# Wider weight slices, gates ahead of values, and earlier loads in a fused attention and SwiGLU kernel

## The chip, the cores and the metric

The kernel runs on one core of one Trainium2 chip. The metric is the device time of one execution in microseconds; lower is better. The core has PE (matmul; PEld is its weight load), DVE, ACT, POOL and SP. SP and POOL issue the DMAs here, and 16 DMA engines serve both queues.

## The reference

The input has 8 batches, 8 heads, 576 positions and a head size of 64. The attention is linear: q gets a softmax over the head size and k one over the sequence; `kv` is k transposed times v; and the output is q times `kv`. The result, 4608 tokens of 512 columns, goes through a gated feed-forward layer with 1536 hidden columns.

```python
q_s = np.exp(q); q_s = q_s / np.sum(q_s, axis=-1)       # softmax, maxima left out here
k_s = np.exp(k); k_s = k_s / np.sum(k_s, axis=2)
x = einsum('bhsd,bhde->bhse', q_s, einsum('bhsd,bhse->bhde', k_s, v))   # -> 4608 x 512
g = x @ w_gate
out = (g * sigmoid(g) * (x @ w_val)) @ w_out
```

Inputs and the output are float32.

## The kernel before

**Weights.** `w_slice` and `wo_slice` load the three weight matrices with DMAs issued from POOL; on the way, the DMA turns float32 into float16. The gate and value weights come in column slices (256, 256, 512 and 512), a slice of the gate and then the same slice of the value matrix. Then w_out comes in three slices of four row tiles of 128. They are listed in `w_dma`, and the first waits for v of batch 0.

**Attention.** A batch is two groups (G) of four heads. `load` brings q, k or v of one group to SBUF from SP's queue, 576 KB each. `exp` is an activation on ACT (`eq`, `ek`). `norm_sum` (`ns`) sums on DVE, `norm_mul` multiplies by the reciprocals on POOL (`nm`, `nd` with a star) or DVE. `tr` transposes on PE for batches 0 and 1; `tr_dma` does it by a DMA for the later ones. `cast_v` (`cv`) turns v into bf16. `kv` and `kv_kn` (`kk`) form the small matrix and scale it, and `x` (`xz`) or `x_pair` (`xx`) write x, transposed, into the ring `xt`.

**Feed-forward layer.** The tokens of batch 0 (576) are done plainly, by class `First`: step `I m` is the gate product of column tile m (eight matmuls into two PSUM banks, 320 and 256 tokens) and its silu on ACT; step `J m` is the value product and the multiply on DVE that writes the hidden ring `hr`. `Unit` (`O j 1`, `O j 2`) multiplies 128 tokens with the first and second half of w_out. The other tokens come in chunks: one of 448 (`PLAN_0`), then seven of 512. There, four pairs of column tiles (`a` to `g`, with `v`) use Strassen's scheme with seven products in the place of eight; the sums of weights are made by `g_sum` (`Q`, `T`) and `w_sum` (`W`), those of x by `x_sum` (`X`, `Y`). The remaining tiles are plain (`G m` gate, `U m` value). The product with w_out of the chunk before is made by `Quad` (`A` to `H`), with sums of `hr` (`S`, by `h_sum`). In the last chunks six pairs are used and no plain tiles.

**What sets the order.** The whole runs under a manual schedule: the order in the program is the order on each engine's queue, and each engine works its queue in order. The order is written out by hand in plan strings: `PLAN_B` (batch 0's layer, attention of batch 1 and the start of batch 2), `PLAN_0` (the 448 tokens), `PLAN` (chunks 1 to 5), `PLAN_N` (6 and 7) and `PLAN_E` (the last product). `op` reads a token, and `chunk` walks a plan. A star moves part of a step to another engine: for `a`, `c`, `d` the copy from ACT to DVE, for `e` and `g` the multiply from POOL to DVE, for `nm` and `Q` from POOL to DVE, for `nd`, `X`, `Y` and `W` from DVE to POOL. `silu` is a tiny activation that brings ACT's table in ahead of its use.

**Buffers.** The PSUM pool `psp` has eight banks, one tile each. The pool `ff` has four buffers `sg` for silu results. `ld` has three buffers for q and k and two for v. `add_manual_dep` adds a wait between two DMAs: before, q of batch 1 waits for `w_dma[-3]`, the first slice of w_out, and k, v of batch 1 and all of batch 2, group 0, follow it on SP's queue.

Of the kernel before, what the change touches and what calls it, by code (L numbers as in the profile page):

```python
# [8 lines left out]
FP32 = mybir.dt.float32  # L9
BF16 = mybir.dt.bfloat16  # L10
FP16 = mybir.dt.float16
AF = mybir.ActivationFunctionType
SYNC = mybir.DependencyInfo(mybir.DependencyClass.Sync, mybir.DependencyReason.DATA)
# [3 lines left out]
def kernel(  # L17
# [19 lines left out]
    nc = tc.nc  # L37

    B, H, S, D = q.shape
# [17 lines left out]
    ff = ctx.enter_context(tc.tile_pool(name="ff", bufs=4))  # L57
# [7 lines left out]
    wg = const.tile([128, KT, d_ff], FP16, name="wg", tag="wg")  # L65
    wv = const.tile([128, KT, d_ff], FP16, name="wv", tag="wv")
# [6 lines left out]
    hr = const.tile([128, MT, RING], BF16, name="hr", tag="hr")  # L73
# [6 lines left out]
    def load(b, G, what, src, after=None):  # L80
        raw[what, b, G] = ld.tile(
            [128, 2, T * 64], FP32, tag=what, name=what, bufs=2 if what == "v" else 3
        )
        ap = bass.AP(
            tensor=src.tensor,
            offset=src[b, 4 * G].offset,
            ap=[[T * 64, 128], [2 * HSTR, 2], [1, T * 64]],
        )
        d = nc.sync.dma_start(out=raw[what, b, G], in_=ap)
        if after is not None:  # L90
            tc.add_manual_dep(d.ins, after.ins.name, SYNC, reason="order of loads")
        dmas[what, b, G] = d
# [5 lines left out]
    def w_slice(dst, src, c0, n):  # L98
        ap = bass.AP(
            tensor=src.tensor,  # L100
            offset=src[0, c0].offset,
            ap=[[d_ff, 128], [128 * d_ff, KT], [1, n]],
        )
        return nc.gpsimd.dma_start(out=dst[:, :, c0:c0 + n], in_=ap)  # L104

    def wo_slice(m0, n):
        ap = bass.AP(
            tensor=moe_w_out.tensor,
            offset=moe_w_out[m0 * 128, 0].offset,
            ap=[[d_model, 128], [128 * d_model, n], [1, d_model]],  # L110
        )
        return nc.gpsimd.dma_start(out=wo[:, m0:m0 + n, :], in_=ap)
# [9 lines left out]
    A, Z = BANKS = ((0, 5), (5, 9))  # L122
# [130 lines left out]
    def warm_up(n):  # L253
        ps = f_tile("warm_ps")
        for _ in range(n):
            nc.tensor.matmul(
                out=ps[:, 0:256], lhsT=zero[:, 0:128], rhs=zero, start=True, stop=True
            )
# [41 lines left out]
    class First:  # L300
# [14 lines left out]

        def run(self, step, alt=False):
            if step == "I":
                self.sg = []
                for p_, (c, n) in zip(self.mm(wg, "g_ps"), self.parts):
                    self.sg.append(ff.tile([128, 512], FP32, tag="sg", name="sg"))  # L320
                    nc.scalar.activation(out=self.sg[-1][:, 0:n], in_=p_[:, 0:n], func=AF.Silu)
            else:
                for p_, sg, (c, n) in zip(self.mm(wv, "u_ps"), self.sg, self.parts):
                    nc.vector.tensor_mul(hr[:, self.m, c:c + n], sg[:, 0:n], p_[:, 0:n])

    def g_cols(w, kh, c0, c1):
        return w[:, 2 * kh:2 * kh + 2, :].rearrange("p k (j c) -> p k j c", j=2)[:, :, :, c0:c1]
# [22 lines left out]
            eng.tensor_sub(s[3], a12, s[1])  # L350

    def sg_tile():
        return ff.tile([128, 512], FP32, tag="sg", name="sg")

    class Pair:
        def __init__(self, c0, h, n, tsum, tc0):
# [35 lines left out]
        def run(self, step, alt=False):  # L392
# [7 lines left out]
            elif step == "b":  # L400
                self.y = f_tile("sy")
                self.prod(self.y, self.raw(wg, 1), self.xa(0, 1), True)
            elif step == "c":
                self.w, self.s5 = f_tile("sw"), self.s_tile("s5")
                self.prod(self.w, self.sum(0), xs[0], True)
                copy(ceng, self.s5, self.w[:, 0:w])
            elif step == "v":
                nc.vector.tensor_add(self.s1, self.y[:, 0:w], self.s1)  # L408
                self.sa = sg_tile()
                nc.scalar.activation(out=self.sa[:, 0:w], in_=self.s1, func=AF.Silu)  # L410
            elif step == "d":
                self.s2 = self.s_tile("s2")
                self.prod(self.x, self.sum(1), xs[1])
                copy(ceng, self.s2, self.x[:, 0:w])
            elif step == "e":
                self.prod(self.w, self.raw(wv, 1), xs[3])
                nc.vector.tensor_add(self.s2, self.w[:, 0:w], self.s2)  # L417
                meng.tensor_mul(self.out(0), self.halves(self.sa), self.halves(self.s2))  # L418
            elif step == "f":
                self.prod(self.x, self.sum(2), xs[2])  # L420
                nc.vector.tensor_add(self.s5, self.x[:, 0:w], self.s5)  # L421
            elif step == "g":
                self.prod(self.x, self.sum(3), self.xa(1, 1))
                sb = sg_tile()
                nc.scalar.activation(out=sb[:, 0:w], in_=self.x[:, 0:w], func=AF.Silu)  # L425
                meng.tensor_mul(self.out(1), self.halves(sb), self.halves(self.s5))  # L426

    class Direct:
# [13 lines left out]
        def run(self, step, alt=False):  # L442
            n = self.n
            if step == "G":
                ps = self.mm(wg, "g_ps")
                self.sg = sg_tile()
                nc.scalar.activation(out=self.sg[:, 0:n], in_=ps[:, 0:n], func=AF.Silu)
            else:
                ps = self.mm(wv, "u_ps")
                nc.vector.tensor_mul(  # L450
                    hr[:, self.m, self.rh:self.rh + n], self.sg[:, 0:n], ps[:, 0:n]
                )
# [141 lines left out]
    with tc.manual_schedule():  # L594
# [20 lines left out]
        cast_v(0, 0, nc.scalar)  # L615

        w_dma = []
        for c0, n in ((0, 256), (256, 256), (512, 512), (1024, 512)):
            w_dma.append(w_slice(wg, moe_w_gate, c0, n))
            w_dma.append(w_slice(wv, moe_w_val, c0, n))  # L620
        tc.add_manual_dep(w_dma[0].ins, dmas["v", 0, 0].ins.name, SYNC, reason="order of loads")
        for m0 in (0, 4, 8):
            w_dma.append(wo_slice(m0, 4))

        warm_up(WARM[0])
        for G in range(NG):
# [17 lines left out]
        x(0, 1, A)  # L644
        x(0, 1, Z)

        load(1, 0, "q", q, after=w_dma[-3])
        load(1, 1, "q", q)
        for G in range(NG):
            load(1, G, "k", k)  # L650
            load(1, G, "v", v)
        load_group(2, 0)

# [88 lines left out]
        ORDER = (0, 1, 2, 3, 4, 5)  # L742
        gt2 = [None] * 4
        PLAN_B = """
        I0 J0 I1 I2 J1 J2 I3 J3 I4 I5 J4 J5 I6 I7 J6 I8 Q0* J7 J8 I9 I10 Q2* Q1* J9 eq0:1
        Q3 J10 eq1:1 I11 ns0:1 ns1:1 J11 ek0:1 ek1:1 nd1:1 O01 nd0:1* cv0:1 O11 O02* tr00
        cv1:1 O12 tr10 tr11 kk0:1 eq0:2 cv0:2 load:2 tr01 O21 xz00 kk1:1 xz01* ns0:2 O22
        nm0:2 ek0:2 xz10* O31 cv1:2 xz11 eq1:2 O32 ek1:2
"""
        PLAN_0 = """  # L750
        a0 b0 ns1 load v0 Y0 G4 a1 Y2 Y1* kv U4 c0 d0 G10 f0 b1 c1 Y3 nm1 W0 g0 d1 v1 a2
        e0 f1 e1 b2 c2 g1 d2 W1 v2 U10 a3 f2 G5 b3 g2 v3 e2 c3 d3* xx* e3 U5 f3 W2 X0 X2
        X1 G11 U11 g3* X3 W3
"""
        PLAN = """
        S002 G4 S022 S102 a0 b0 G10 d0 c0 A v0 a1 S042 eq0 S122 S142 S302 B S342 f0 S242
        b1 ek0 U4 S322 D S222 ek1 e0 eq1 cv0 S202 C* v1 cv1 g0 ns0 F E d1 H* a2 ns1 c1 f1
        silu nm0 b2 c2 nm1 e1 g1 d2* v2 a3 U10 f2 e2 load kv b3 g2 c3 d3 G5 v3 e3* f3 xx*
        X0 G11 U5 X1 U11 g3* X3 X2
"""  # L760
        PLAN_N = """
        a0 b0 c0 d0 A v0 T0* f0 S002 a1 b1 g0 d1 c1 S022 S102 S222 v1 e0 a2 S202 f1 e1 b2
        S042 c2 g1 d2 v2 S122 B f2 a3 T1 b3 c3 S242 S142 g2 e2 d3 S322 D v3 a4 f3 T2 C g3
        T3 d4 b4 e3 c4 v4 f4 S302 F a5 g4 b5 S342 d5 v5 e4 c5* f5 E X0 X1 e5* X3 X2* g5*
        H*
"""
        PLAN_E = """
        S202 S042 S022 S002 A S142 S122 S102 B C S322 S302 S342 D S222 S242 E F H*
"""
        chunk(-1, 0, S, PLAN_B)  # L770
        chunk(0, S, 1024 - S, PLAN_0)
# [33 lines left out]
```

## Time and profile before

| what | value |
|---|---|
| median of 5 runs | 302.82 us (301.5 to 304.96) |
| profiled execution, its own time | 304.12 us |
| its span | 302.2 us |
| PE, PEld, DVE, ACT, POOL busy | 290.9, 228.4, 232.4, 210.7, 136.7 us |
| HBM read and written | 37.75 and 9.44 MB |
| q0 (POOL's DMAs), q1 (SP's) | 4.72 and 41.30 MB |

The span is the time between the first and the last record of the profiled execution. Its own time is longer by what lies around the span. A busy time of an engine is the sum of its instructions' times without overlaps. The traffic of q0 is counted as written, in float16, which is half of what is read.

### The profile page before, as it was taken

The page shows a single profiled execution, that of the slowest core. Times are in us where ns is not written, and L with a number is a line of the kernel's source. Part 1 is how long each engine was busy: PE and PEld are TensorE (multiplying, and loading weights), DVE is VectorE, ACT ScalarE, POOL GpSimd, SP SyncE. Part 2 cuts the span into 40 slices and gives each one's busy share as a digit, 9 for nine tenths or more (in the row PEclk, how much of TensorE's full clock was granted, in tenths as well). Part 3 has the DMA queues.
Part 4 walks back from the last instruction along what each step waited for, and adds up shares of the span by engine and source line. Part 5 has one row for each costly group of instructions (what it writes and reads, how often), then busy time and mean ns, then how long its engine had stood idle before and what let it go on. Part 6 is the DMA issues. An engine that isn't in the chain of part 4 may idle for free.

```text
span 302.2 us, 6895 instructions
## 1 busy us (share of the span) xinstructions
PE 290.9 (96%) x2644; PEld 228.4 (76%) x2644; DVE 232.4 (77%) x497; ACT 210.7 (70%) x385; POOL 136.7 (45%) x108
## 2 busy tenths in 40 slices
PE   8999978979999999999999999999999999999993
PEld 6777744558688858885888588858886888888882
DVE  3943846658898878887888788878988898895981
ACT  5654377677889488948894889488948776567540
POOL 1840155456407910791079107910794465274500
PEclk9999997979999999999999999999999999999999
DMA  7999998999001993189317941993190000600066
GB/s 268 267 179 206 236 395 286 303 293 293 0 3 34 177 359 120 34 176 343 139 32 158 335 165 31 190 341 129 30 192 0 0 2 4 135 7 0 2 139 139
DMA packets 38863, 46.43 MB, mean 154 GB/s; under 512 B 16304, under 2 KB 21936, under 8 KB 38832
## 3 DMA queue, kind: packets, MB, share of 16 engines
q1 hardware_dynamic: 33024, 41.30, 47.6%
q0 software_dynamic: 5808, 4.72, 10.2%
q8 instruction: 20, 0.33, 0.5%
q14 instruction: 11, 0.09, 0.1%
HBM read 37.75 MB, written 9.44 MB: 156 GB/s over the span
## 4 chain that ended last, share of the span: by engine, by line
PE 79%; DMA 13%; POOL 2%; SPq 1%; ACT 1%; DVE 1%; issue 0%; ACTq 0%; POOLq 0%; DVEq 0%
PE sx L384 21%; PE ox L526 14%; PE sw L384 10%; PE u_ps L435 7%; PE ow L526 7%; PE g_ps L435 7%; DMA wo<-in_moe_w_out_dram 5%; DMA v<-in_v_dram 5%; PE sy L384 5%; PE oy L526 3%; DMA q<-in_q_dram 2%; PE kv L192 2%; POOL wg L104 1%; PE o_ps L473 1%; POOL wv L104 1%; DVE rs L143 1%
## 5 line engine op out<-in xcount | busy, mean ns | idle before, releaser
L418 POOL TENSOR_TENSOR hr<-sg,s 128x512 bf16<-128x512 f32 (+1 forms) x29 | 38.0, 1309 | 74.7 <-DVE s L417 73.5
L384 PEld LDWEIGHTS <-gt 128*128 128x128 f16 x576 | 56.6, 98 | 11.0 <-issue 0.7
L426 POOL TENSOR_TENSOR hr<-sg,s 128x512 bf16<-128x512 f32 (+1 forms) x28 | 35.7, 1274 | 36.9 <-ACT sg L425 36.9
L384 PE MATMUL sx<-xs,gt 128*128 128x256 f16 (+1 forms) x288 | 43.1, 273 | 0.0
L116 ACT COPY s<-sx 128x512 f32<-128x512 f32 (+1 forms) x66 | 38.2, 579 | 5.2 <-PE sx L384 4.4
L526 PEld LDWEIGHTS <-hs 128*128 128x128 bf16 x384 | 37.6, 98 | 5.4
L417 DVE TENSOR_TENSOR s<-sw,s 128x512 f32<-128x512 f32 (+1 forms) x36 | 24.5, 681 | 16.5 <-PE sw L384 16.2
L425 ACT ACTIVATE sg<-sx 128x512 f32<-128x512 f32 (+1 forms) x36 | 21.2, 590 | 19.9 <-PE sx L384 14.7
L152 POOL TENSOR_TENSOR qs<-eq,rr 128x1152 bf16<-128x1152 bf16 x14 | 29.5, 2127 | 11.4 <-DVE rr L147 11.4
L421 DVE TENSOR_TENSOR s<-sx,s 128x512 f32<-128x512 f32 (+1 forms) x36 | 24.4, 679 | 10.0 <-PE sx L384 4.8
L384 PEld LDWEIGHTS <-wg 128*128 128x128 f16 x288 | 27.7, 98 | 5.2
L526 PEld LDWEIGHTS <-hr 128*128 128x128 bf16 x288 | 28.1, 98 | 3.3
L143 DVE TENSOR_REDUCE rs<-eq 128x18 f32<-128x1152 bf16 x16 | 21.5, 1341 | 10.0 <-ACT eq L127 10.0
L410 ACT ACTIVATE sg<-s 128x512 f32<-128x512 f32 (+1 forms) x36 | 22.5, 626 | 8.0 <-DVE s L408 7.9
L116 ACT COPY s<-sw 128x512 f32<-128x512 f32 (+1 forms) x34 | 19.8, 584 | 9.9 <-PE sw L384 4.9
L408 DVE TENSOR_TENSOR s<-sy,s 128x512 f32<-128x512 f32 (+1 forms) x36 | 24.3, 674 | 1.3 <-ACT s L116 0.8
L435 PE MATMUL g_ps<-xt,wg 128*128 128x512 f16 (+1 forms) x96 | 24.5, 378 | 0.0
L435 PE MATMUL u_ps<-xt,wv 128*128 128x512 f16 (+1 forms) x96 | 24.1, 384 | 0.0
L526 PE MATMUL ox<-wt,hs 128*128 128x256 f16 x192 | 23.6, 273 | 0.0
L384 PE MATMUL sw<-xs,gt 128*128 128x256 f16 (+1 forms) x144 | 21.8, 275 | 0.0
L384 PE MATMUL sy<-xt,wg 128*128 128x256 f16 (+1 forms) x144 | 21.4, 271 | 0.0
L384 PE MATMUL sx<-xt,gt 128*128 128x256 f16 (+1 forms) x144 | 21.4, 271 | 0.0
(99 smaller groups left out, 570.8 us busy)
## 6 DMA issues: line engine op xcount, KB each, us to landing
q<-in_q_dram SPq DMA_DIRECT2D x16, 576.0 KB, 6.7
k<-in_k_dram SPq DMA_DIRECT2D x16, 576.0 KB, 8.0
v<-in_v_dram SPq DMA_DIRECT2D x16, 576.0 KB, 8.6
out_dram<-o_sb SPq DMA_DIRECT2D x72, 128.0 KB, 2.4
wo<-in_moe_w_out_dram POOLq DMA_DIRECT2D x3, 512.0 KB, 18.4
wg<-in_moe_w_gate_dram POOLq DMA_DIRECT2D x2, 512.0 KB, 11.0
wv<-in_moe_w_val_dram POOLq DMA_DIRECT2D x2, 512.0 KB, 12.7
wg<-in_moe_w_gate_dram POOLq DMA_DIRECT2D x2, 256.0 KB, 6.1
```

The lines of the kernel that those rows point to most:

```text
L116: nc.scalar.copy(out=out, in_=in_)
L143: nc.vector.reduce_sum(out=rs, in_=s["eq"].rearrange("p t h d -> p (t h) d"), axis=mybir.AxisListType.X)
L152: eng.tensor_mul(s["qs"].rearrange("p t (h d) -> p (t h) d", d=64), s["eq"].rearrange("p t h d -> p (t h) d"), s["rr"].to_broadcast([128, ...
L384: nc.tensor.matmul(out=bank[:, h * j:h * j + h], lhsT=wgt(kk, j), rhs=rhs[:, kk, 0:h], start=first and j == 0 and kk == 0, stop=kk == 1, s ...
L408: nc.vector.tensor_add(self.s1, self.y[:, 0:w], self.s1)
L410: nc.scalar.activation(out=self.sa[:, 0:w], in_=self.s1, func=AF.Silu)
L417: nc.vector.tensor_add(self.s2, self.w[:, 0:w], self.s2)
L418: meng.tensor_mul(self.out(0), self.halves(self.sa), self.halves(self.s2))
L421: nc.vector.tensor_add(self.s5, self.x[:, 0:w], self.s5)
L426: meng.tensor_mul(self.out(1), self.halves(sb), self.halves(self.s5))
L435: nc.tensor.matmul(out=ps[:, 0:self.n], lhsT=w[:, kk, 128 * self.m:128 * self.m + 128], rhs=xt[:, kk, self.r:self.r + self.n], start=(kk = ...
L526: nc.tensor.matmul(out=dst[p][:, 0:HN], lhsT=lhs(kk, p), rhs=rhs(kk), start=start and i == 0, stop=i == HM - 1, skip_group_check=True,)
```

## The change

1. The gate and value weights come in three slices of 512 columns each (before: 256, 256, 512, 512).
2. In `First`, the silu results of one step go into two parts of one `sg` tile of 576 columns; before, into two tiles of 512. The four buffers are then enough for four steps. The tile is as wide in the other classes, which use the same columns of it as before.
3. q of batch 1, both groups, is issued on SP's queue after the fourth weight slice has landed (before: after the first slice of w_out). The first slice of w_out waits on POOL's queue for the fifth weight slice. k of batch 1 waits for the sixth on SP's queue.
4. `PLAN_B` runs the gates up to four steps ahead of the values, and puts the attention of batches 1 and 2 elsewhere among them. `kv`, the load of the next batch and the sums stand elsewhere in `PLAN_0`. `PLAN`, `PLAN_N` and `PLAN_E` have the same steps in another order and with other stars.

```diff
             if step == "I":
-                self.sg = []
-                for p_, (c, n) in zip(self.mm(wg, "g_ps"), self.parts):
-                    self.sg.append(ff.tile([128, 512], FP32, tag="sg", name="sg"))
-                    nc.scalar.activation(out=self.sg[-1][:, 0:n], in_=p_[:, 0:n], func=AF.Silu)
+                ps = self.mm(wg, "g_ps")
+                self.sg = ff.tile([128, S], FP32, tag="sg", name="sg")
+                for p_, (c, n) in zip(ps, self.parts):
+                    nc.scalar.activation(
+                        out=self.sg[:, c:c + n], in_=p_[:, 0:n], func=AF.Silu
+                    )
             else:
-                for p_, sg, (c, n) in zip(self.mm(wv, "u_ps"), self.sg, self.parts):
-                    nc.vector.tensor_mul(hr[:, self.m, c:c + n], sg[:, 0:n], p_[:, 0:n])
+                for p_, (c, n) in zip(self.mm(wv, "u_ps"), self.parts):
+                    nc.vector.tensor_mul(
+                        hr[:, self.m, c:c + n], self.sg[:, c:c + n], p_[:, 0:n]
+                    )
...
     def sg_tile():
-        return ff.tile([128, 512], FP32, tag="sg", name="sg")
+        return ff.tile([128, S], FP32, tag="sg", name="sg")
...
-        for c0, n in ((0, 256), (256, 256), (512, 512), (1024, 512)):
+        for c0, n in ((0, 512), (512, 512), (1024, 512)):
             w_dma.append(w_slice(wg, moe_w_gate, c0, n))
             w_dma.append(w_slice(wv, moe_w_val, c0, n))
         tc.add_manual_dep(w_dma[0].ins, dmas["v", 0, 0].ins.name, SYNC, reason="order of loads")
+        load(1, 0, "q", q, after=w_dma[3])
+        load(1, 1, "q", q)
         for m0 in (0, 4, 8):
             w_dma.append(wo_slice(m0, 4))
+        tc.add_manual_dep(w_dma[6].ins, w_dma[4].ins.name, SYNC, reason="order of loads")
...
-        load(1, 0, "q", q, after=w_dma[-3])
-        load(1, 1, "q", q)
         for G in range(NG):
-            load(1, G, "k", k)
+            load(1, G, "k", k, after=w_dma[5] if G == 0 else None)
             load(1, G, "v", v)
         load_group(2, 0)
...
         PLAN_B = """
-        I0 J0 I1 I2 J1 J2 I3 J3 I4 I5 J4 J5 I6 I7 J6 I8 Q0* J7 J8 I9 I10 Q2* Q1* J9 eq0:1
-        Q3 J10 eq1:1 I11 ns0:1 ns1:1 J11 ek0:1 ek1:1 nd1:1 O01 nd0:1* cv0:1 O11 O02* tr00
-        cv1:1 O12 tr10 tr11 kk0:1 eq0:2 cv0:2 load:2 tr01 O21 xz00 kk1:1 xz01* ns0:2 O22
-        nm0:2 ek0:2 xz10* O31 cv1:2 xz11 eq1:2 O32 ek1:2
+        I0 I1 I2 I3 J0 J1 J2 J3 I4 J4 I5 J5 I6 I7 J6 eq0:1 J7 Q0* Q1 I8 I9 ns0:1 I10
+        nd0:1* J8 I11 cv0:1 cv1:1 J9 J10 J11 O01 Q2* O11 eq1:1 ek0:1 ns1:1 O02 tr00 ek1:1
+        tr01 nd1:1 O21 kk0:1 O12 tr10 load:2 tr11 Q3 xz00* eq0:2 kk1:1 xz01 O31 xz11*
+        ek0:2 cv0:2 ns0:2 O22 xz10* cv1:2 nm0:2* O32 eq1:2 ek1:2
         PLAN_0 = """
-        a0 b0 ns1 load v0 Y0 G4 a1 Y2 Y1* kv U4 c0 d0 G10 f0 b1 c1 Y3 nm1 W0 g0 d1 v1 a2
-        e0 f1 e1 b2 c2 g1 d2 W1 v2 U10 a3 f2 G5 b3 g2 v3 e2 c3 d3* xx* e3 U5 f3 W2 X0 X2
-        X1 G11 U11 g3* X3 W3
+        Y0 Y2 Y1 a0* ns1 G4 G10 U4 b0 d0 c0 v0 a1 U10 Y3* f0 nm1 b1 c1 e0 g0 W0 d1 v1 e1
+        a2 f1 b2 v2 kv W1* g1 d2 G5 c2 f2 xx e2 a3 g2 load G11 d3 W3 b3 c3 v3 U5 f3 e3* X0
+        U11 g3 X2 X1 X3 W2
         PLAN = """
-        S002 G4 S022 S102 a0 b0 G10 d0 c0 A v0 a1 S042 eq0 S122 S142 S302 B S342 f0 S242
-        b1 ek0 U4 S322 D S222 ek1 e0 eq1 cv0 S202 C* v1 cv1 g0 ns0 F E d1 H* a2 ns1 c1 f1
-        silu nm0 b2 c2 nm1 e1 g1 d2* v2 a3 U10 f2 e2 load kv b3 g2 c3 d3 G5 v3 e3* f3 xx*
-        X0 G11 U5 X1 U11 g3* X3 X2
+        S042 G4 S002 U4 S102 ek0 a0 S222 b0 S022 A eq0 B S142 d0 S122 c0 eq1 S202 G10 f0
+        S342 C S322 D v0 e0 a1 S242 g0 S302 ns0 ek1 cv0 ns1 cv1 b1 F U10 c1 nm1 d1 E silu
+        nm0 H* v1 a2 f1 kv g1 d2 b2 c2 v2 a3 f2 e1 b3 c3 g2 e2 d3 v3 load e3 G5 f3 xx X2
+        X0 G11 X1 U5 g3 U11 X3
         PLAN_N = """
-        a0 b0 c0 d0 A v0 T0* f0 S002 a1 b1 g0 d1 c1 S022 S102 S222 v1 e0 a2 S202 f1 e1 b2
...
+        a0 b0 T0 c0 d0 A v0 S042 f0 S022 a1 b1 g0 S002 T1 d1 c1 v1 e0 a2 f1 e1* b2 c2 S102
...
         PLAN_E = """
-        S202 S042 S022 S002 A S142 S122 S102 B C S322 S302 S342 D S222 S242 E F H*
+        S042 S002 S022 S142 S122 A S222 S102 S302 S202 S322 S342 B C S242 D E F H*
```

More of the change, by code (lines that the diff above doesn't have):

```diff
@@ L760 @@
+        nm0 H* v1 a2 f1 kv g1 d2 b2 c2 v2 a3 f2 e1 b3 c3 g2 e2 d3 v3 load e3 G5 f3 xx X2
+        X0 G11 X1 U5 g3 U11 X3
 """
         PLAN_N = """
-        a0 b0 c0 d0 A v0 T0* f0 S002 a1 b1 g0 d1 c1 S022 S102 S222 v1 e0 a2 S202 f1 e1 b2
-        S042 c2 g1 d2 v2 S122 B f2 a3 T1 b3 c3 S242 S142 g2 e2 d3 S322 D v3 a4 f3 T2 C g3
-        T3 d4 b4 e3 c4 v4 f4 S302 F a5 g4 b5 S342 d5 v5 e4 c5* f5 E X0 X1 e5* X3 X2* g5*
-        H*
+        a0 b0 T0 c0 d0 A v0 S042 f0 S022 a1 b1 g0 S002 T1 d1 c1 v1 e0 a2 f1 e1* b2 c2 S102
@@ L766 @@
+        g1 d2 v2 B f2 S122 T2 a3 S142 b3 g2 d3 c3 v3 e2 S342 a4 f3 b4 v4 D S242 g3 S222 T3
+        d4 S322 e3 c4 C S202 f4 a5* F g4 d5 b5 c5 S302 e4 v5 f5 X2* E e5* X0 X1 g5* X3* H*
 """
         PLAN_E = """
-        S202 S042 S022 S002 A S142 S122 S102 B C S322 S302 S342 D S222 S242 E F H*
+        S042 S002 S022 S142 S122 A S222 S102 S302 S202 S322 S342 B C S242 D E F H*
 """
```

## The prediction, made blind

> **What bounds the kernel now.** I read the page's busy line first (PE 290.9 of 302.2 us, 96%), then PE's idle time among the waits, the windows by stage, the chain of waits, and the timelines of ACT and SP. The busy share says that only PE's holes and its slow stretches are to be had; the other views say where they are.
>
> ```profile
> PE 290.9 (96%) x2644; PEld 228.4 (76%) x2644; DVE 232.4 (77%) x497; ACT 210.7 (70%) x385; POOL 136.7 (45%) x108
> PEclk9999997979999999999999999999999999999999
> ```
> PE misses 11.3 us in all, and the granted clock dips twice, in slices 7 and 9 (45 to 53 and 60 to 68 us).
>
> ```profile
> PE o_ps L473 <- DVE hr L324: 2.6, 1, 2.6
> PE kv L192 <- POOL vb L118: 1.7, 1, 1.7
> ```
> Those are PE's two long waits (waited for: us, times, longest).
>
> ```profile
> 16.07:39.60 23.53, 23.53 (x192) 18.80 (x193) 13.20 (x30) 9.65 (x25) 5.62 (x6) 1.00 1.23 227
> 39.60:57.95 18.35, 15.70 (x120) 7.33 (x117) 12.15 (x26) 13.59 (x17) 9.77 (x6) 0.91 0.94 320
> 57.95:70.00 12.05, 10.32 (x98) 7.62 (x97) 7.48 (x18) 8.91 (x14) 5.14 (x5) 0.86 1.08 320
> ...
> 102.69:132.97 30.28, 30.28 (x282) 23.55 (x284) 25.00 (x56) 23.91 (x43) 13.91 (x11) 1.00 0.63 169
> ```
> Columns: length, then busy us of PE, PEld, DVE, ACT, POOL, then clock, DMA share, GB/s. Batch 0's gates and values (16 to 39.6) run without a hole, at 23.53/24 = 0.98 us a step. The holes and the lower clock lie between 39.6 and 70. A later chunk is full, so reordering it can hardly gain.
>
> ```profile
> 32.98 6.91 DMA q<-in_q_dram
> 39.96 1.28 ACT L127
> 41.25 1.17 ACT eq L127
> 42.45 1.36 DVE rs L143
> 44.17 1.22 DVE rs L143
> 45.59 0.44 DVE hr L324
> 46.08 0.56 PE o_ps L473
> ...
> 52.91 8.32 DMA v<-in_v_dram
> 61.38 1.15 POOL vb L118
> 62.58 0.70 PE kv L192 x18
> ```
> The chain gives both causes. Batch 1's q waits for the first w_out slice (16.38 + 16.6 = 32.98), lands at 39.9, and ACT stands at eq in front of I11's silu; J11's multiply, and the second half of w_out's product, wait for that. Later v of batch 2, group 1, issued at 52.91, holds kv.
>
> ```profile
> 39.96 1.28 ACT L127 ACT_TABLE_LOAD   x1 [3.47 <-DMA q<-in_q_dram]
> ```
>
> [...] 2 us windows from 44 on have clocks 1.00, 0.54, 0.60, 1.00, which is 3.4 us at half speed after the hole of 2.65, and 0.81, 0.50, 0.84 from 62 on, 3.4 us again after the hole of 1.72. Each costs 1.7 us of matmul. [...] the trace has 1.28 us and the activation directly behind it, so I use 1.28. [...] loads issued from 32.98 on left the rate at 206 GB/s, the weights' own, until 36 (337 in 36 to 38), so about two queued slices of weights went first.
>
> **The change, part by part**, in the time of the profiled execution.
>
> *512-column slices.* Issue to landing gives the landings of before: gate 16.03, value 16.66, gate 18.5, value 19.8 (256 columns each), then 22.4, 24.9, 28.0, 30.5, with w_out at 33.0, 35.6, 39.7. Bytes in order: the first new slice holds what had landed by 16.66, so I0 starts at 16.7 instead of 16.07, **+0.65**. Bounds: 0 [...], +2.4 (as late as the third old slice). The values then have 3.9 us more cover, since I0 to I3 come first. Their four gates take all 8 PSUM banks, but I0's silu is over at 18.6 and J0 starts at 20.6. Steps at 0.98: I4 24.5 (slice 22.4), J4 25.5 (24.9, 0.6 to spare), I8 32.4, J8 35.3, end 40.2. The two 320/256 silus into one 576-wide tile cost nothing: the operations are the same, and the four buffers now hold four gates instead of two.
>
> *q of batch 1 after the fourth slice.* Issued at 24.9 with two slices queued, the state of 32.98; so it lands 6.9 us later, at 31.8. ACT is free at 31.2 (I7's silu): table 33.1, eq 34.25, table 35.55, I8's silu 36.2, when I11 takes that bank at 36.3. It just fits; a later q costs PE the excess. The last slices are slowed by the q loads: 27.5 to 30.4 and about 31.6, against 32.4 and 35.3. Two loads take 3.0 us of DMA (six landed 1.5 apart from 39.9 to 47.6).
>
> *w_out after the fifth slice, k and v after the sixth.* POOL now waits in front of w_out until about 28; behind it stand Q1 (needs DVE's Q0, 34.5), nd0 and the v casts, none due before 34. Remaining bytes end near 45.5: w_out lands around 33, 37, 41 (O02 needs the last at 42.8; 44.5 if the queues alternate evenly), v at 42.6 and 45.6. SP's k issue waits for the sixth slice with v, q, k of the next group behind it, none due before 41.
>
> *PLAN_B.* POOL: Q1 34.5 to 39.1 (2 x 2.3, row of gt), nd0 to 41.2, casts 43.8 and 46.8. O01, O11 cover J11's multiply. Then tr00 44.1 (qs 41.2), kk0 46.0 (cast 43.8), tr10 47.9 (nd1 about 47.0), kk1 48.8 (cast 46.8), xz11 50.9 (kn 50.8). The hole of 2.65 and its 1.7 of half speed go: **-4.35**. The stage is 18.35 - 4.35 = 14.0 and ends at 54.2 instead of 57.95.
>
> *PLAN_0.* kv moves from the fifth PE step to behind some twenty, so v is covered: **-3.4** (1.72 + 1.7). What is late next is ACT. SP issues q, k, v of group 1 behind O12's stores (copy 48.5), from 49.7; with 5.5 to 7.4 us to landing k is there at 56.5 to 57.7. ek is done at 57.7 to 58.9, then table 1.28, silus of G4 and G10 (0.5 each), the copy of d0 (0.5): f0, which adds to the bank that this copy reads, starts at 60.5 to 61.7. PE has 4.95 us of other work and is there at 59.0. I take **+1.5** (bounds 0.5 and 3). [...] W1 goes to POOL (estimate 3.3 us, from 1.11 us for 448 columns), and holds g1, e2 and so G11's buffer and d3's copy: **+0.5** (0 to 1.2) at f3.
>
> *PLAN, five chunks.* ACT gets two more table loads per chunk, 2.56 us (ek0, eq0, eq1, then silu, ek1, silu; before, exp came in one group). Walking ACT with 1.07 (exp), 0.47 (copy), 0.49 (silu): d0's copy ends at 6.7 and f0 is at 7.0; D's copies 11.2, F 11.8; a2's copy 19.4, d2 19.9. Never late, by 0.25 at the least. DVE loses C, d2, e3, g3 and gets xx. PE's own work is 66560 columns at 0.109 us per 256, 28.4, with kv 1.15 and xx 0.54 30.1 of 30.28. **0**, bounds -0.2 and +2.3 each. PLAN_N and PLAN_E keep their PE work (27.6 per chunk, full) and the tail after the last matmul: 0.
>
> Sum: 0.65 - 4.35 - 3.4 + 1.5 + 0.5 = **-5.1**. The profiled execution took 304.12 (span 302.2), so 299.0 in its like; from the median 302.82, **297.7**.
>
> **Rivals.**
> - *Nothing takes the holes' place* (0.09): k lands before 55.5 and neither f0 nor f3 waits: -5.1 - 2.0 = 295.7. For it: no loads stand in front of it. Against: before, the same three took 6.6 to 8.3 us.
> - *The loads move the hole* (0.22): w_out's last slice at 44.5 stops O02 for 1.7, and f0's hole drops the clock for 1.7: 297.7 + 3.4 = 301.1. For it: before, a hole of 1.72 did just that. Against: the weights that were queued went first.
> - *Slower: ACT becomes the bound of the five full chunks* (0.16). The 2.56 us of table loads stand in front of d0's copy, on which f0 waits. With 0.25 to spare they cost nothing; of each us by which ACT is later than I walked it, all is PE time, five times. At 1.27 us later the whole gain is gone; at 1.75, five times 1.5 gives 297.7 + 7.5 = 305.2; the full 2.56 would give 309. For it: PE has no slack there to give back. Against: ACT is busy 23.9 of 30.28, and 26.5 still fits.
>
> **How the numbers follow.** My case has 0.53 and 297.7, with its own 295.8 to 300.5 from the bounds above. A measurement of this kernel tells about 1% (3 us; its runs were 301.5 to 304.96). Faster by over 1% (below 299.8): 0.50 of mine, 0.09, 0.06 of the second rival: 0.65. Within: 0.03, 0.14 and 0.01: 0.18. Slower: 0.02 and 0.15: 0.17. The range leaves out most of the slower case and the far end of the best: 295.0 to 303.5.
>
> **What would show it.** Right: I0 at 16.5 to 17; eq within the gates with no wait of over 1 us in front of it; no PE wait on hr before O02 and none on vb at kv; no half-speed slice near 46; the first 512-column gate of chunk 1 at 75 to 76.5 instead of 80.7; the five chunks still 30.1 to 30.4; a PE hole at f0 near 59. Wrong: I8, J8 or O02 waiting for weights, chunks over 30.6 with ACT in front of f0 or F, or a third hole in the place of the two.

## The result, and the profile after

The changed kernel takes 305.45 us (median of 44 runs, 302.76 to 308.79), the kernel before 302.96 us beside it (79 runs). The ratio of the times is 1.0073, 95% interval 1.0058 to 1.0088: slower by 0.7%, some 2 us, where 297.7 us was forecast. The profiled span is 303.6 us, against 302.2 before.

The profile of the changed kernel is of an execution near its median (305.42 us), but that of before is of a longer one (304.12 us, mean clock 0.989): of the 77 executions of before timed beside the experiments, 53 had a mean clock of 0.991 or more and a median of 302.8 us, the other 24 a median of 305.4.

The page's busy line and clock line after:

```profile
PE 289.5 (95%) x2644; PEld 227.9 (75%) x2644; DVE 227.3 (75%) x492; ACT 219.8 (72%) x391; POOL 149.3 (49%) x115
PEclk9999997999999999999999999999999999999999
```

TensorE now misses 14.1 us of its span, before 11.3. One of the two dips of the clock is gone, the one in slice 9. Where the new holes are, the waits of TensorE tell (us in total, times, longest):

```profile
PE o_ps L477 <- DMA wo<-in_moe_w_out_dram: 3.4, 1, 3.4
PE sx L388 <- ACT s L116: 1.9, 3, 1.3
PE g_ps L310 <- DMA wg<-in_moe_w_gate_dram: 1.2, 1, 1.2
...
PE xa L273 <- DMA qtd<-qs: 0.8, 2, 0.4
```

The waits on hr before O02 and on POOL's vb at kv have gone. In the place of the first stands a longer one, at the same O02, for w_out itself. The windows by stage (columns as before: batch 0's gates and values; the rest of PLAN_B; PLAN_0; chunks 1 to 4):

```profile
17.29:40.82 23.53, 23.53 (x192) 18.80 (x193) 11.73 (x26) 14.95 (x30) 8.40 (x6) 1.00 1.19 252
40.82:59.73 18.91, 15.50 (x121) 7.63 (x118) 12.29 (x26) 8.05 (x13) 9.34 (x6) 0.91 0.81 248
59.73:80.04 20.31, 18.98 (x197) 15.11 (x196) 16.86 (x36) 16.10 (x30) 15.17 (x10) 1.00 0.88 266
80.04:110.33 30.29, 30.29 (x283) 23.56 (x282) 26.17 (x58) 26.50 (x45) 16.27 (x12) 1.00 0.37 77
110.33:141.12 30.79, 30.36 (x282) 23.57 (x281) 24.43 (x54) 25.96 (x44) 16.35 (x12) 1.00 0.60 168
141.12:171.44 30.32, 30.32 (x282) 23.55 (x280) 23.73 (x55) 26.19 (x46) 16.32 (x12) 1.00 0.60 172
171.44:202.66 31.22, 30.60 (x282) 23.53 (x280) 23.99 (x54) 25.96 (x44) 16.33 (x12) 1.00 0.60 175
```

Stage by stage the difference to the profile of before is (PLAN_0 begins at its first matmul in both profiles; in that of before this is at 58.16, 0.21 us after the boundary 57.95 used ahead of the result):

| stage | before, us | after, us | difference | forecast |
|---|---|---|---|---|
| start of the first gate (I0) | 16.07 | 17.29 | +1.22 | +0.65 |
| batch 0's gates and values | 23.53 | 23.53 | 0 | 0 |
| rest of PLAN_B | 18.56 | 18.91 | +0.35 | -4.35 |
| PLAN_0, to chunk 1's first 512-column gate | 22.57 | 20.31 | -2.26 | -1.4 |
| chunks 1 to 5, to the last plain gate of chunk 5 | 148.38 | 150.35 | +1.97 | 0 |

The differences add up to +1.3, against +1.4 of the spans. Two terms carry the miss: the rest of PLAN_B (4.7 us worse than forecast) and the five chunks (2.0).

The chain of waits shows the first cause:

```profile
29.16 18.22 DMA wo<-in_moe_w_out_dram
47.38 0.04 issue
47.42 1.87 PE o_ps L477 x4
```

w_out's last slice is under way for 18.2 us. O02 stops from 44.0 to 47.42, and the half-speed stretch follows (clock 0.50 in the window from 47 to 49). The loss is the old one with a new owner.

### The profile page after: what moved, and what is told of

Its sections match the earlier page's. It is cut to its first block, busy times and chain, and to the rows that moved or that the text cites. A ratio compares the mean times of both kernels' runs of the same rounds, so it can differ in the third digit from the quotient of the medians.

```text
span 303.6 us, 6922 instructions
## 1 busy us (share of the span) xinstructions
PE 289.5 (95%) x2644; PEld 227.9 (75%) x2644; DVE 227.3 (75%) x492; ACT 219.8 (72%) x391; POOL 149.3 (49%) x115
## 4 chain that ended last, share of the span: by engine, by line
PE 67%; DMA 20%; POOL 3%; SPq 2%; DVE 2%; ACT 2%; issue 1%; ACTq 0%; POOLq 0%; DVEq 0%
PE sx L388 18%; PE ox L530 13%; PE sw L388 8%; PE ow L530 6%; DMA wo<-in_moe_w_out_dram 6%; PE u_ps L439 5%; PE g_ps L439 5%; DMA wg<-in_moe_w_gate_dram 5%; PE sy L388 4%; DMA k<-in_k_dram 4%; PE oy L530 3%; DMA v<-in_v_dram 3%; DMA qtd<-qs 3%; PE kv L192 2%; SPq L466 2%; PE o_ps L477 2%
## 5 line engine op out<-in xcount | busy, mean ns | idle before, releaser
L422 POOL TENSOR_TENSOR hr<-sg,s 128x512 bf16<-128x512 f32 (+1 forms) x31 | 40.7, 1321 | 64.6 <-ACT sg L414 42.2
L388 PEld LDWEIGHTS <-gt 128*128 128x128 f16 x576 | 55.7, 98 | 14.7 <-issue 3.4
L430 POOL TENSOR_TENSOR hr<-sg,s 128x512 bf16<-128x512 f32 (+1 forms) x34 | 42.8, 1258 | 33.3 <-ACT sg L429 33.1
L116 ACT COPY s<-sx 128x512 f32<-128x512 f32 (+1 forms) x69 | 40.1, 582 | 3.5 <-PE sx L388 2.0
L429 ACT ACTIVATE sg<-sx 128x512 f32<-128x512 f32 (+1 forms) x36 | 21.6, 601 | 15.7 <-PE sx L388 11.3
L152 POOL TENSOR_TENSOR qs<-eq,rr 128x1152 bf16<-128x1152 bf16 x13 | 27.4, 2125 | 6.0 <-DVE rr L147 6.0
L116 ACT COPY s<-sw 128x512 f32<-128x512 f32 (+1 forms) x36 | 21.1, 586 | 7.5 <-PE sw L388 7.5
L118 POOL CAST vb<-v 128x1152 bf16<-128x1152 f32 x14 | 15.9, 1156 | 13.6 <-PE sw L388 8.7
```

Of the source, the lines that this page charges most:

```text
L116: nc.scalar.copy(out=out, in_=in_)
L152: eng.tensor_mul(s["qs"].rearrange("p t (h d) -> p (t h) d", d=64), s["eq"].rearrange("p t h d -> p (t h) d"), s["rr"].to_broadcast([128, ...
L388: nc.tensor.matmul(out=bank[:, h * j:h * j + h], lhsT=wgt(kk, j), rhs=rhs[:, kk, 0:h], start=first and j == 0 and kk == 0, stop=kk == 1, s ...
```

## The experiments

All are timed against the kernel before. In the five chunks I count from chunk 1's first 512-column gate to the last plain gate of chunk 5, 148.38 us before and 150.35 after.

**1. Is it the added wait of w_out?** The changed kernel without it:

```diff
-        tc.add_manual_dep(w_dma[6].ins, w_dma[4].ins.name, SYNC, reason="order of loads")
```

> The changed kernel without the wait of w_out's first slice for the fifth weight slice: w_out is queued behind the weights at once, as before the change. Theory [...]: its three slices land by about 40, O02 does not wait, the half-speed stretch of 3.4 us goes, and the kernel gains 3.4 + 1.7 = 5.1 us against the changed one, about 300.4. Rival (the total of bytes sets the time, so something else arrives late in its place, q or v of batch 1): under 1.5 us gained, with a PE hole of 2 us or more at another step before 62 us.

Measured: 305.18 us, ratio 1.0065 (1.0042 to 1.0088). w_out is issued from 14.5 us on instead of 27.7, and O02 still waits for it, 3.36 us, until 47.01. The added wait is not the cause. w_out's last slice lands at 46.97 without it and at 47.38 with it, so its place on POOL's queue is not what delays it.

**2. The changed kernel with PLAN of the kernel before.** Only chunks 1 to 5 are put back.

```diff
-        S042 G4 S002 U4 S102 ek0 a0 S222 b0 S022 A eq0 B S142 d0 S122 c0 eq1 S202 G10 f0
+        S002 G4 S022 S102 a0 b0 G10 d0 c0 A v0 a1 S042 eq0 S122 S142 S302 B S342 f0 S242
...
```

> The changed kernel with PLAN, the order of chunks 1 to 5, as before the change; all else as changed. Theory (the new order of the five full chunks costs 2.0 us: from the start of chunk 1 to that of chunk 6 the traces show 153.4 us after and 151.4 before): 2 us less than the changed kernel, 303.4, with five chunks of 30.3. Rival (the loss is all ahead of chunk 1, and what the chunks lose they lose to a late start of their loads there): no gain, 305.4.

Measured: 303.48 us, ratio 1.0006 (0.9978 to 1.0034), five chunks 148.51. The new order of PLAN explains the net loss; the other parts, with their hole at O02, cancel to zero within the interval.

**3. The kernel before with the new PLAN alone**, the opposite edit.

```diff
-        S002 G4 S022 S102 a0 b0 G10 d0 c0 A v0 a1 S042 eq0 S122 S142 S302 B S342 f0 S242
+        S042 G4 S002 U4 S102 ek0 a0 S222 b0 S022 A eq0 B S142 d0 S122 c0 eq1 S202 G10 f0
...
```

> The kernel before with only PLAN changed. Theory: 2.0 us slower than before, 305.0, with waits of the transposes' users (xa) and of d0 or f0 on ACT's copies in some chunks. Rival (the chunks lose only because PLAN_0 of the change hands over late loads): within 0.5 us of before.

Measured: 305.59 us, ratio 1.0073 (1.0048 to 1.0099), five chunks 150.78. The loss is the same without any of the other parts. Over all profiles the five chunks take 148.38 to 148.51 us with the old PLAN (six profiles) and 149.57 to 150.78 with the new one as it stands (four).

Ahead of the chunks this kernel is the kernel before, so its profile is a second look at it. The hole at O02 is there as before, 2.66 us. At kv there is less:

```profile
PE kv L192 <- POOL vb L118: 0.6, 1, 0.6
```

No half-speed stretch follows (four matmuls of 224 columns take 0.55 us together behind this hole, where in the profile of before they took 0.95), and PLAN_0 takes 20.89 us instead of 22.57. So the second hole of 1.72 us and the halved clock behind it belong to the one execution that was profiled, and not to every execution of before.

**4. The changed kernel with narrow first slices.**

```diff
-        for c0, n in ((0, 512), (512, 512), (1024, 512)):
+        for c0, n in ((0, 256), (256, 256), (512, 512), (1024, 512)):
```
(The waits on `w_dma` are moved two places on, to the same slices.)

> The changed kernel with the first slices at 256 columns again (each wait moved to the slice with the same bytes). Theory (I0 started at 17.29 instead of 16.07 since the first wide slice is twice the bytes and its first packets were slow): I0 at 16.1 to 16.3 and the gates' end 1.1 us earlier. Whether that reaches the end depends on w_out: if O02 waits for a DMA that is no earlier, the kernel gains nothing (305.4); if it does come earlier, 1.2 us (304.2).

Measured: 306.8 us, ratio 1.0115 (1.0081 to 1.0148). (The first packets of the changed kernel's wide slices did come slowly: 36 started from 12 to 13 us, 128 and 190 in the next two, 206 from 16 to 17.) I0 starts at 15.40, but the stage ends at 39.92, as it waits for later slices, and O01 and O02 then wait 1.33 and 3.39 us for w_out. This is no gain, so the wide slices are not what costs.

**5. Both transposes ahead of the stores.** In chunk 4 of the changed kernel SP's queue reads (start, duration, all us):

```profile
191.22 1.31 SPq L180 DMA_TRANSPOSE qtd<-qs  x1
192.63 2.47 SPq L466 DMA_DIRECT2D out_dram<-o_sb  x4
195.20 1.31 SPq L180 DMA_TRANSPOSE qtd<-qs  x1
196.61 2.47 SPq L466 DMA_DIRECT2D out_dram<-o_sb  x4
199.13 0.58 SPq L89 DMA_DIRECT2D q<-in_q_dram  x1
199.76 0.49 SPq L89 DMA_DIRECT2D k<-in_k_dram  x1
```

Before, in the same chunk, it reads:

```profile
186.65 5.50 SPq L462 DMA_DIRECT2D out_dram<-o_sb  x8
192.26 2.75 SPq L180 DMA_TRANSPOSE qtd<-qs  x2
195.06 0.58 SPq L89 DMA_DIRECT2D q<-in_q_dram  x1
```

The new PLAN makes E and H later, and so the block on SP, which is full from 191.22 to 203.3, and the loads at its end. POOL had finished the second transpose's input by 193.3; the transpose stood behind four stores.

```diff
-  ... c1 nm1 d1 E silu nm0 H* v1 ...
+  ... c1 nm1 nm0 d1 E silu H* v1 ...
```

> The changed kernel with one token of PLAN moved: nm0 directly behind nm1, so that both DMA transposes of a chunk are on SP ahead of the eight output stores; the six loads stay last. In the changed kernel the second transpose is issued at 195.20, behind four stores, though GpSimd had its input at 193.3. Theory 'SP carries the loss': the second transpose goes about 1.9 us earlier, the waits of PE for qtd (0.8 and 1.6 us over the chunks) go, and the median falls by 1 to 1.6 us, to about 304.1; ek still waits for k (1.1 us in chunk 4), so a loss of about 1 us against the kernel before stays. Rival 'the longer order on ScalarE (four table loads a chunk) carries it': within 0.3 us of the changed kernel's 305.4.

Measured: 305.61 us, ratio 1.0078 (1.005 to 1.0105): no gain. TensorE's waits for qtd are gone, but the loads came no earlier (chunk 4: q at 199.86), and ScalarE's waits for k doubled from 1.3 to 2.6 us. Who waits for the tile k between 80 and 240 us, in the changed kernel and in this one:

```profile
  ACT ek L127: 1.3, 2
```

```profile
  ACT ek L127: 2.6, 3
```

The five chunks take 150.47. ek0 stands ahead of a0's copy in ScalarE's order and waits for k; d0 waits for that copy. The expected gain of 1 to 1.6 us did not come: the wait for k took over what the transposes gave back. The number is the one that the rival named, but its reason, the table loads, is tested only by 6. The waits of TensorE that the profile lists in the chunks (1.4 us in the changed kernel, 1.1 here) cover only a part of the loss; the rest does not show as a wait.

**6. Transposes, then loads, then stores.**

```diff
-  ... c1 nm1 d1 E silu nm0 H* v1 ... v3 load e3 ...
+  ... c1 nm1 nm0 load d1 E silu H* v1 ... v3 e3 ...
```

> The changed kernel with nm0 and the six loads directly behind nm1 in PLAN, so SP issues both transposes, then the loads, then the eight stores; the order on TensorE, and the four table loads a chunk on ScalarE, stay. Theory 'SP carries the loss': waits for qtd and for k both go, the five chunks take 30.3 us each as before, and the median is 303.3 to 303.6, the 2 us of the chunks being regained. Rival 'ScalarE carries it': it stays within 0.3 us of 305.4 with waits of TensorE for copies on ScalarE. Should the stores, now last, hold the o_sb tiles too long, the copies into o_sb wait and part is given back.

Measured: 303.25 us, ratio 0.9983 (0.9953 to 1.0013). SP's queue in chunk 4 (between 80 and 240 us nobody waits for k or qtd):

```profile
188.98 3.37 SPq L180 DMA_TRANSPOSE qtd<-qs  x2
192.40 0.59 SPq L89 DMA_DIRECT2D q<-in_q_dram  x1
193.04 0.47 SPq L89 DMA_DIRECT2D k<-in_k_dram  x1
...
196.04 9.69 SPq L466 DMA_DIRECT2D out_dram<-o_sb  x8
```

The five chunks take 148.38 us, to the hundredth what they took before, with the four table loads a chunk, 1.28 us each in the changed kernel, still in place (ScalarE busy 219.7 us). From 5 to 6 the loads alone were moved, and the loss went. So the loss of the chunks lies in the order on SP's queue, and the table loads cost nothing here. What the loads alone would give, with the transpose left where it was, no run shows.

**7 and 8. w_out without the company of k and v.** Both have before's PLAN, so that the stages up to chunk 1 are seen alone; but for one line they are the kernel of 2, 303.48 us. k of batch 1, with all that follows it on SP, waits for w_out's last slice (7) or its second (8):

```diff
-            load(1, G, "k", k, after=w_dma[5] if G == 0 else None)
+            load(1, G, "k", k, after=w_dma[8] if G == 0 else None)
```
(In 8 it is `w_dma[7]`.)

> The changed kernel with PLAN of the kernel before, and the loads of k, v of batch 1 and of batch 2 held until the last slice of w_out has landed. Theory 'w_out is late because k and v share the DMA engines with it': w_out's last slice lands at about 39 to 41 instead of 47, the hole of O02 (3.3 us) and the half-speed stretch behind it (1.7 us) go, and the median falls from 303.5 to about 299 if the later k and v (landing at about 46 to 51) still fit. Rival 'the hole only moves': kk0 or kk1 waits 2 to 4 us for k or v, with a half-speed stretch again, and the median is 302 to 304.

> As the kernel with k held until w_out's last slice, but held until its second slice only, so k and v share the engines with one slice of w_out. Theory 'k and v share the engines': the last slice lands at about 42 to 44, O02 waits less than 1 us and no half-speed stretch follows, 299 to 300. Rival 'the hole only moves': a wait at O02 of 1 to 2 us with a half-speed stretch, 302 to 303.

Measured: 300.11 us, ratio 0.9898 (0.9867 to 0.9929), and 299.34 us, ratio 0.9883 (0.9846 to 0.992). O02 waits in neither. w_out's times from issue to landing (us, min/median/max), in the changed kernel and in 8:

```profile
DMA to landing us min/median/max: 8.1/13.1/18.2
```

```profile
DMA to landing us min/median/max: 7.9/9.8/11.5
```

The slices land at 35.83, 41.55 and 47.38 in the changed kernel, at 34.69, 37.29 and 39.78 here: 5.7 and 5.8 us apart with k, v and q beside them, 2.6 and 2.5 with k held. The sharing is the cause. When k is held to the last slice (7), kv waits 1.66 us for its v; held to the second (8), it doesn't. In both, f0 now waits for ScalarE, 2.08 and 2.54 us; in 8 the clock is 0.50 behind it, from 62 to 64 us. The profile of 8 is of an execution of 301.02 us, 1.7 above its median.

**9. The next cover: batch 2's loads.** In 8 f0 stands behind a chain that the waits of ScalarE show: q and k of batch 2, group 1, issued from 49.76 on behind the stores of the first output units; eq and ek wait 1.4 and 0.4 us for them; then the table load, two Silus and d0's copy. One token of PLAN_B moves, on top of 8:

```diff
-  ... O11 eq1:1 ek0:1 ns1:1 O02 tr00 ... O12 tr10 load:2 tr11 ...
+  ... O11 eq1:1 ek0:1 ns1:1 load:2 O02 tr00 ... O12 tr10 tr11 ...
```

> The kernel with k held until w_out's second slice (before's PLAN), with one token of PLAN_B moved: load:2 ahead of O02, so q, k and v of batch 2's second group stand on SP ahead of the output stores of the first units and not behind them. In the kernel it starts from they were issued at 49.76 to 50.98 and ScalarE's exps at the end of the stage waited 1.4 and 0.4 us for them, which made d0's copy late and f0 wait 2.5 us, with a half-speed stretch (1.7 us lost) behind it. Theory 'the chain is load, exp, copy, f0': q and k are issued at about 46, f0's wait falls below 1 us, the half-speed stretch goes, and the median falls from 299.3 to 296 to 297. Rival 'the order on ScalarE alone (table load, two Silus and copies behind two exps) makes f0 late': f0 still waits 1.5 us or more and the median stays within 1 us of 299.3.

Measured: 297.75 us, ratio 0.9811 (0.9764 to 0.9859). It has the lowest median of all and is faster than the kernel before and the changed one; its interval just overlaps that of 8, though each of its six executions (up to 298.26) is shorter than each of 8's (from 298.87). q is issued at 45.71, eq and ek of this group wait for nothing, f0 waits 0.56 us, and TensorE's waits are down to:

```profile
...
PE sx L388 <- ACT s L116: 0.6, 1, 0.6
PE g_ps L310 <- DMA wg<-in_moe_w_gate_dram: 0.3, 1, 0.3
```

The rest of PLAN_B, in its windows, takes 14.47 us at full clock; the forecast had 14.0:

```profile
39.28:53.75 14.47, 14.18 (x120) 7.14 (x118) 12.01 (x26) 8.17 (x13) 8.04 (x6) 1.00 1.04 387
```

**10. The same with the narrow slices of 4**, the waits again moved to the same slices.

```diff
-        for c0, n in ((0, 512), (512, 512), (1024, 512)):
+        for c0, n in ((0, 256), (256, 256), (512, 512), (1024, 512)):
```

> The same with the first two column slices of the weights 256 wide again. Theory 'wide first slices cost their later landing': the First stage begins about 1.3 to 1.9 us earlier, of which 0.4 to 1.0 us comes back as waits for slices within the stage, so 0.3 to 0.9 us less than the kernel with the load moved. Rival 'the next load takes its place': O02 then waits for w_out's last slice, by as much or more (with a half-speed stretch, up to 2 us slower).

Measured: 299.01 us, ratio 0.9843 (0.9796 to 0.989). Here too the narrow slices bring no gain: I0 starts 0.26 us earlier than in 9, the stage ends 0.58 later, and kv then waits 1.66 us for vb. The interval overlaps that of 9, so whether they lose is not settled. The rival of this run was right in kind, but what took the place was v and not w_out.

## Why the prediction was wrong

*w_out after the fifth slice, k and v after the sixth: the step that failed first.* The prediction put w_out's last slice at 41, with 44.5 "if the queues alternate evenly", and took 41. It landed at 47.4. Two estimates went wrong. The first slice landed at 35.8 and not at 33 (34.7 even with k held, in 8). And from there the queues did share: in the trace's DMA records between 35 and 43 us w_out's packets (1024 bytes) and those of q, k and v (2304 bytes) went about one for one, some 90 of each per us (182 on each queue from 39 to 41). A slice of 512 KB has 512 such packets, 5.7 us at that rate, which is the measured spacing; with k held it took 2.5 to 2.6. The even sharing alone would have brought the 44.5 of the prediction: by 44.0 all but 45 of w_out's 1536 packets had started. These last ones went at 9 to 23 per us, until 46.8, and the slice landed at 47.38. Which of the 16 engines held them, and why they fell behind, no view shows. The prediction had set the even sharing aside in part because of three microseconds of the trace of before, in which the weights already queued went ahead. That head start is there again: k was issued at 31.56, and from 33 to 35 the cast weights still had the engines nearly alone, with 412 packets against 5, at 207 GB/s. Even sharing is what the counts show from 35 to 43, with both queues well under way, and no more than that was shown. The rival "The loads move the hole" named this cause and this place, but with 1.7 us; it was 3.4, and a half-speed stretch came behind it.

*PLAN_B.* The reordered gates and values, q in time (eq at 33.14 with no wait in front of it) and the cover of J11's multiply were right. -4.35 became +0.35 through w_out: once w_out came in time (9), the stage took 14.47 us, -4.1.

*PLAN, five chunks: the step that failed second.* Its 0 was worked out by walking ScalarE, DVE and TensorE. SP's queue was not walked, though the step makes the stores later, puts the transposes between them and leaves the six loads behind them (in chunk 4 the loads begin at 199.13 instead of 195.06). That cost 1.97 us, and 2 and 3 show that it makes up the net loss against the kernel before. The rival that forecast slower chose the same chunks and the wrong cause: with four table loads a chunk and the loads earlier (6) nothing was lost. In the changed kernel ScalarE was late because k was late (in chunk 4 ek waited 1.1 us for it).

*PLAN_0: the price of kv, the step that failed third.* kv's hole went, and f0's new hole was 1.32 us against the 1.5 taken, for the reason given. W1 took 3.1 us on POOL (3.3 estimated), but the 0.5 for it can't be told apart. Against the profile of before the stage gave -2.26, 0.9 better than the -1.4. But the -3.4 for kv, a hole of 1.72 us and 1.7 for the halved clock, was read from one execution. In the profile of 3, with the same PLAN_0 as before, kv waits 0.64 us at full clock, and against that one the stage gave only -0.6. That -1.4 lies between the two is luck. The last line of the sum then took this price from the median, whose executions mostly had too high a mean clock for two half-speed stretches (two of 3.4 us at half speed take 0.011 off the mean over 302.2 us; the profiled execution, which has two, stands at 0.989).

*512-column slices.* The +1.22 of the profile is mostly scatter between executions. Over the eight profiles with wide slices O01 starts from 39.28 to 40.82, on average 40.07; over the four with narrow ones from 39.37 to 39.92, on average 39.69. That leaves +0.4, or +0.6 against the two narrow ones that also have the old order of gates (39.37 and 39.60): near the +0.65.

Summed up, the forecast had -5.1 us for the stages and they gave +1.3, a gap of 6.4: 4.7 from the rest of PLAN_B, 2.0 from the five chunks and 0.6 from the slices, less 0.9 from PLAN_0. The median was missed by more, 7.7 us (305.45 against 297.7). The other 1.3 is the step from the profiled execution, 304.12, down to the median, 302.82.

## What to carry to other kernels

When a reordering moves stores, transposes and loads that are issued from one queue, walk that queue as an engine of its own, up to the load at its end: here the next chunk's exp waited there. Before you send loads earlier, list what else is on its way in those microseconds and which of it is due first; here two queues under way together started 182 packets each from 39 to 41 us, and holding the load that was due later was worth more than issuing everything early. When a hole doesn't close, look at who owns it now: here the reordering of PLAN_B was worth nearly its forecast, but only after the transfer behind it was freed. And before you put a price on a hole, ask whether the profiled execution is like the median one; a second profile of the same stage can tell.

## What the runs showed of the hardware

- The second slice of w_out, cast on its way, landed 2.6 us after the first when the loads of k and v were held (8, 208 GB/s), and 5.7 us after it beside the loads of q, k and v (294 GB/s in all). The sharing cost the cast transfer more than half its rate, while the total rose.
- In these runs a hole's length alone did not tell whether half speed follows. Before, the clock was 0.50 from 64 to 66 us behind one of 1.72 us; in 7 one of 2.08 us at f0 and one of 1.66 at kv passed at full clock, and in 8 one of 2.54 us at f0 did not:

```profile
60.00:62.00 2.00, 0.55 (x3) 0.20 (x2) 0.25 (x1) 1.99 (x3) 1.77 (x2) 1.00 0.76 221
62.00:64.00 2.00, 1.37 (x15) 1.37 (x15) 1.97 (x4) 1.96 (x6) 2.00 (x2) 1.00 0.00 0
```

```profile
60.00:62.00 2.00, 0.22 (x3) 0.21 (x3) 1.10 (x3) 1.99 (x5) 2.00 (x3) 0.99 0.57 180
62.00:64.00 2.00, 2.00 (x13) 1.65 (x11) 1.21 (x3) 1.08 (x3) 1.61 (x1) 0.50 0.00 0
```

  (Windows around f0 in 7, then in 8; the third number from the end is the clock.) The half-speed stretches behind holes in the profiles of before (two) and of the changed kernel (one) last 3.4 us each by their clock records. What else decides whether one follows was not shown; no run moved a hole on purpose.
